# Sparse attention, then Sinkhorn-routed experts on one core: weight loads ordered behind row copies and x, masks and clears moved to GpSimd

## The chip, the cores and the metric

The kernel runs on one core of a Trainium2 chip. The time is device microseconds of one execution, lower is better. The engines are TensorE (PE in the profile; PEld is its weight load), VectorE (DVE), ScalarE (ACT), GpSimd (POOL) and SyncE (SP). DMAs here are issued from the queues of POOL (loads from memory, which also convert f32 to 16 bits), of SP (copies inside the core's memory, transpositions, stores) and at a few places of ACT.

## The reference

Attention over 4 x 8 heads of 768 rows and 64 columns: each query sees the keys closer than 16 rows and a maximum of each block of 32 keys (with the mean of that block's values, weighted by 32). Its result, 3072 rows of 512, goes through eight experts; the gate's probabilities are balanced by eight rounds of row and column scaling.

```python
k_sum = k.reshape(B, H, nb, block, D).max(axis=3)
v_sum = v.reshape(B, H, nb, block, D).mean(axis=3)
mask_l = np.abs(pos[:, None] - pos[None, :]) < window
scores_s = scale * einsum('bhsd,bhnd->bhsn', q, k_sum) + np.log(block)
a = softmax(concat([where(mask_l, scale * q @ k.T, -1e9), scores_s]))
x = matmul(a, concat([v, v_sum]))          # then rows of 512
P = np.exp(x @ w_gate - max)
for _ in range(8):
    P /= P.sum(1, keepdims=True) + 1e-09
    P /= P.sum(0, keepdims=True) + 1e-09
    P *= N / E
for e in range(E):
    out += P[:, e:e + 1] * (np.maximum(x @ w1[e], 0.0) @ w2[e])
```

## The kernel before

**Stages.** Heads go in 16 pairs. Pairs 0 to 3 (the first batch) are done in halves (`pair_half`), pairs 4 to 15 whole (`pair_whole`). Expert 0 is computed as plain matmuls on 384 rows at a time (`hidden0` L221, `project0` L231) while attention runs. Experts 1 to 7 follow in a loop of 80 equal steps with Strassen-like products (L972, L978) whose sums and differences are made on DVE (L919, L922); the first four groups of expert 1 and the eight rounds of scaling (`bridge`, L1159) share the time with the last rows of expert 0.

**Order.** Attention, expert 0 and the bridge are not issued in program order. `Plan` (L35) takes units with an engine, a cost in microseconds, dependences and a priority, and always emits the unit that can start first. So the costs written into `add(...)` decide the order in which each engine's queue is filled; in the run each engine goes through its queue in that order. A unit may have several engines to choose from. DMAs are units of their own: an issue on POOL, a transfer on one "DMA" resource, a landing some time later (`load`, L670); `last[0]` chains all POOL units in a fixed order. `plan.idle` puts filler matmuls (L592) where the plan sees PE free for more than 0.22 us, until the first eviction of expert 0.

**One whole pair** (`pair_whole`, L756). K and Q are transposed (PE, L349; from pair 12 on by a DMA transposition from SP, L354). `key_max` (L370) makes the maxima of 32 keys in three DVE operations (L375 to L377). `block_sums` (PE, L393) and `block_out` (DVE, L399) make the block means of the values in rows 0 to 63 of a tile `V_e`, group 0; L405 spreads them over the other groups. Rows 64 to 127 of `V_e` hold copies of value rows just outside each group of 128: `near_values` (L409), four small DMAs on SP (L414, L416, 10.2 KB each). Scores (PE, L383), exponential (ACT, L429) and band masks (DVE, L435) follow; `edges` (L439) masks the 16 columns on each side of a group into a tile `E_e`, four DVE operations of 32x80. `values` then multiplies: L458 with the own group's values, L464 with `E_e` and `V_e`. `normalize` (DVE, L546 and L547) gives `xs`; x is transposed into `xT` on PE, or for pairs 10 to 14 by a DMA transposition on SP (`x_dma`, L358). There are two `V_e`, two `E_e` and two `xs` tiles, used in turn.

**Clears and constants.** `pads(n)` (L613) clears the gaps of three mask tiles `E_h`; `gate_constants` (L649) casts the identity and the gate's weights; `late_constants` (L653) clears `E_e`, `V_e` and sets `col_en`. All on DVE.

**The end of attention on POOL.** `hold` (L883) copies one element of each of four `qT` tiles to `held`, which makes POOL wait for the Q of pairs 12 to 15; behind it stand the loads of expert 1: four blocks of w1 (`load_w1`, L197, two DMAs each) and w2 (`load_w2`, L208). The sums of those blocks (`w1_sum`, units `Wt` in `bridge`) are DVE units whose dependences in the plan do not name the loads.

Of the kernel before, what the change touches and what calls it, by code (L numbers as in the profile page):

```python
# [10 lines left out]
BF16 = mybir.dt.bfloat16  # L11
# [125 lines left out]
def kernel(  # L137
# [110 lines left out]
    if True:  # L248

        ident = attn.tile([128, 128], BF16, name="ident")  # L250
        held = attn.tile([1, 1], BF16, name="held")
        band = attn.tile([128, LIVE], BF16, name="band")
# [117 lines left out]
        def key_max(i):  # L370
            r = i % NB
            km = attn.tile([128, 1, 24], BF16, tag="km", name="km", bufs=2)
            half = attn.tile([128, 24, 16], BF16, tag="kh", name="kh", bufs=1)
            rows = kT[r][:].rearrange("p (n w) -> p n w", w=32)
            nc.vector.tensor_tensor(out=half[:], in0=rows[:, :, 0:16], in1=rows[:, :, 16:32], op=ALU.max)  # L375
            nc.vector.tensor_tensor(out=half[:, :, 0:8], in0=half[:, :, 0:8], in1=half[:, :, 8:16], op=ALU.max)
            nc.vector.tensor_reduce(out=km[:, 0, :], in_=half[:, :, 0:8], axis=AX.X, op=ALU.max)  # L377
            nc.vector.tensor_tensor(out=ksT[r][:, 0:64].rearrange("p (j n) -> p j n", j=2)[:, :, 0:24],
                                    in0=km[:].to_broadcast([128, 2, 24]), in1=own[:, :, 0:24], op=ALU.mult)
# [16 lines left out]
        def block_out(i):  # L396
            vs = at.pop(("vs", i))
            dst = V_s[i] if i < PB else V_e[i % NE][:, 0, :]
            nc.vector.tensor_tensor(  # L399
                out=dst[0:64].rearrange("p (j x) -> p j x", j=2)[:, :, 0:D],  # L400
                in0=vs[0:64].rearrange("p (j d) -> p j d", j=2),
                in1=own[0:64, :, 24:25].to_broadcast([64, 2, D]), op=ALU.mult)
            if i >= PB:
                ve = V_e[i % NE]
                nc.vector.tensor_copy(out=ve[0:64, 1:G, :],  # L405
                                      in_=ve[0:64, 0:1, :].to_broadcast([64, G - 1, 2 * VD]))

# [31 lines left out]
        def edges(i):  # L439
            ee, er = E_e[i % NE], at.pop(("er", i))  # L440
            for j in range(2):
                q0 = 64 + 32 * j
                nc.vector.tensor_tensor(out=ee[q0:q0 + 32, 0:G - 1, 128 - W:128],
                                        in0=er[0:32, j, 1:G, 0:W],
                                        in1=band[0:32, None, 0:W].to_broadcast([32, G - 1, W]),
                                        op=ALU.mult)
                nc.vector.tensor_tensor(out=ee[q0:q0 + 32, 1:G, 0:W],
                                        in0=er[96:128, j, 0:G - 1, W + 128:LIVE],
                                        in1=band[96:128, None, W + 128:LIVE].to_broadcast([32, G - 1, W]),
                                        op=ALU.mult)  # L450

# [46 lines left out]
        def live(c):  # L498
            return PAD + c * (LIVE + PAD)
# [102 lines left out]
        def band_constants():  # L602

            nc.gpsimd.affine_select(out=band, in_=band, compare_op=ALU.is_ge, fill=0.0,
                                    base=-1, pattern=[[1, LIVE]], channel_multiplier=-1)
            nc.gpsimd.affine_select(out=band, in_=band, compare_op=ALU.is_ge, fill=0.0,
                                    base=2 * W - 1, pattern=[[-1, LIVE]], channel_multiplier=1)

        def ident_constant():
# [3 lines left out]
        def pads(n):  # L613
            t = E_h[n]
            nc.vector.memset(t[:, :, 0:PAD], 0.0)
            nc.vector.memset(t[:, :, live(0):live(HG)].rearrange("p j (g l) -> p j g l", l=LIVE + PAD)[:, :, :, LIVE:],
                             0.0)
            nc.vector.memset(t[:, :, live(HG) + W:], 0.0)

# [28 lines left out]

        def gate_constants():  # L649
            nc.vector.tensor_copy(out=ident16[:], in_=ident[:])  # L650
            nc.vector.tensor_copy(out=wg_bf[:], in_=wg_f32[:])

        def late_constants():  # L653
            def zero(t):
                nc.vector.memset(t, 0.0)

            def ones(t):
                nc.vector.memset(t[0:24, :, D:VD], 32.0 / XS)
                nc.vector.memset(t[32:56, :, VD + D:2 * VD], 32.0 / XS)

            parts = [(0.4, lambda t=t: zero(t[64:128, :, :])) for t in E_e]
            for t in V_e:
                parts += [(0.4, lambda t=t: zero(t[:])), (0.15, lambda t=t: ones(t))]
            return parts + [(0.15, lambda: nc.vector.memset(col_en, float(E) / float(N)))]

# [22 lines left out]
        def pair_start(i, prio):  # L688
# [17 lines left out]
            if i < PB:  # L706
                query_half(i, 0, prio)
            U["km", i] = add("DVE", 0.85, lambda: key_max(i), [U["kT", i, 0]] + war_q[2:], prio)
            if i == 0:
                U["gc"] = add("DVE", 0.35, gate_constants, [U["km", 0]], 0.5)  # L710
# [3 lines left out]
            U["Vs", i] = add("DVE", 0.24 if i < PB else 0.7, lambda: block_out(i), [U["vs", i]],  # L714
                             prio + 0.01, uses=[buf])
# [10 lines left out]
        def pair_half(i, h, prio):  # L726
            if h:
                query_half(i, 1, prio)
            n = PB * h + i
            hold = U["A", PB - 1, 0] if h else None  # L730
            clear = add("DVE", 0.65, lambda: pads(n), [U["km", n - 1]], prio - 0.2) if 0 < n < NEH else None
            buf = Buffer("s")
# [3 lines left out]
            U["mk", i, h] = add("DVE", 0.78, lambda: masks_h(i, h),  # L736
                                [U["X", i, h], U["band"], hist("A", n - NEH), clear], prio)
            tag = "a" if h else "m"
# [17 lines left out]
        def pair_whole(i, prio):  # L756
            U["near", i] = add("SP", 2.5, lambda: near_values(i), [U["v", i], U.get(("A", i - NE, 1))], prio,
                               lag=4.5)
            for h in range(2):
# [5 lines left out]
                                    [U["X", i, h], U.get(("A", i - 2, 1))], prio)  # L765
            U["ed", i] = add("DVE", 0.78, lambda: edges(i),
                             [U["X", i, 0], U["X", i, 1], U["mk", i, 1], U.get(("A", i - NE, 1))], prio)
# [5 lines left out]
            for h in range(2):  # L773
                buf = Buffer("a")
                U["A", i, h] = add("PE", 0.36, lambda h=h: values(i, h),
                                   [U["mk", i, h], U["ed", i], U["sx", i, h], U["Vs", i], U["near", i]],
                                   prio, opens=[buf])
# [49 lines left out]
        def gate(b, xs, prio):  # L827
            buf = Buffer("a")
            U["lg", b] = add("PE", 0.61, lambda: logits(b), xs, prio, opens=[buf])
            U["lo", b] = add("ACT", 0.25, lambda: logits_out(b), [U["lg", b]], prio, uses=[buf])  # L830
# [13 lines left out]
        load_pair(1, "k0")  # L844
        U["band"] = last[0] = add("POOL", 0.7, band_constants, [last[0]])
        load_pair(1, "v")
        load_pair(2, "k0")
        load_pair(3, "k0")
        load_pair(2, "v")
        load_pair(3, "v")  # L850
        zero_w1(0)
        for i in range(PB):
            load_pair(i, "1")
        zero_w1(1)
        load("w2", lambda: load_w2(0), 0.85, 5.2)
        U["gc"] = None
        for i in range(PB):
            pair_start(i, i)
            pair_half(i, 0, i)
        c1 = U["x", PB - 1, 0]  # L860
        for us, fn in late_constants():
            c1 = add("DVE", us, fn, [c1], 12.5)
        expert0(0, [U["x", i, 0] for i in range(PB)])
# [40 lines left out]
    if True:  # L904
# [254 lines left out]
        def bridge():  # L1159
# [54 lines left out]
            for i in range(4):  # L1214
# [8 lines left out]

                op("p1", "PE", 0.44, [], [a])
                op("seed", "ACT", 0.58, ["p1"], [g], [a])
# [133 lines left out]
```

## Time and profile before

| | us |
|---|---|
| median of three runs | 671.15 |
| the runs | 670.29, 671.15, 671.94 |
| the profiled execution | 674.88 |
| its span (first to last instruction) | 673.2 |
| PE busy | 661.4 |
| DVE busy | 581.9 |
| ACT busy | 399.7 |
| POOL busy | 129.5 |

The page lists groups of instructions by line, engine and tile: `out<-in`, shape, count, then busy time and mean duration. Busy time by stage (the first number is the stretch's length, then each engine's busy time with its instructions, the granted TensorE clock, the DMA engines' share and GB/s):

```profile
0.00:15.00 15.00, 13.03 (x166) 7.07 (x168) 11.95 (x84) 9.15 (x15) 13.95 (x24) 1.00 1.43 155
15.00:50.00 35.00, 34.56 (x468) 23.33 (x463) 29.09 (x89) 25.78 (x45) 27.32 (x34) 1.00 1.97 169
50.00:100.00 50.00, 49.27 (x537) 30.44 (x536) 46.06 (x139) 35.32 (x58) 31.38 (x42) 1.00 1.76 129
100.00:150.00 50.00, 46.86 (x348) 26.36 (x347) 35.93 (x104) 27.79 (x53) 6.57 (x11) 0.97 0.46 51
150.00:190.00 40.00, 40.00 (x247) 23.99 (x247) 30.97 (x71) 26.79 (x52) 6.91 (x10) 1.00 0.25 34
```

Attention ends in the fourth stretch; the fifth goes over into the equal steps of experts 1 to 7. The share in the DMA column adds up packets that overlap and can be above 1.

### The profile page before, as it was taken

To read this page: it belongs to the slowest core of one execution; us is meant where nothing else is said; L and a number is where in the kernel's file an instruction comes from. 1 tells how busy PE (TensorE), PEld (TensorE's weight loads), DVE (VectorE), ACT (ScalarE), POOL (GpSimd) and SP (SyncE) were. 2 spreads that over 40 slices of the span, in tenths; PEclk is the share of its full clock that TensorE was granted. 3 is DMA by queue.
4 is the path that set the end of the run, shared out by engine and by line. 5 is a ranking of instruction groups with operands and counts; after the bars stand their busy time and mean duration, and the time that the engine had idled before them with its cause. 6 is when DMAs were issued, how large, how long until landed. Compare 5 with 4: busy or idle time off the path is not lost.

```text
span 673.2 us, 13510 instructions
## 1 busy us (share of the span) xinstructions
PE 661.4 (98%) x5077; PEld 436.4 (65%) x5077; DVE 581.9 (86%) x1475; ACT 399.7 (59%) x782; POOL 129.5 (19%) x175
## 2 busy tenths in 40 slices
PE   8999998999999999999999999999999999999996
PEld 4766655555666666666666666666666666666665
DVE  8889897677799988998799988998899879998885
ACT  6776674565777765555655565555555565556551
POOL 8699440122101010201010010101020101100001
PEclk9999999999999999999999999999999999999999
DMA  9999989000513050311422051305031132201224
GB/s 159 184 150 147 143 97 142 1 1 1 78 11 39 1 79 1 36 14 20 61 23 25 1 79 12 37 1 79 1 36 14 27 52 23 26 1 56 86 80 157
DMA packets 124033, 36.75 MB, mean 55 GB/s; under 512 B 110144, under 2 KB 121152, under 8 KB 123968
## 3 DMA queue, kind: packets, MB, share of 16 engines
q0 software_dynamic: 104128, 25.93, 41.3%
q1 hardware_dynamic: 18880, 9.22, 6.7%
q8 instruction: 40, 0.66, 0.4%
q10 hardware_dynamic: 960, 0.74, 0.3%
q14 instruction: 25, 0.20, 0.1%
HBM read 52.45 MB, written 6.29 MB: 87 GB/s over the span
## 4 chain that ended last, share of the span: by engine, by line
PE 88%; DVE 6%; DMA 5%; issue 0%; ACT 0%; DVEq 0%; ACTq 0%
PE xy L978 37%; PE pg L972 16%; PE pa L972 11%; PE pb L972 11%; PE yps L231 5%; PE hps L221 4%; DMA Ve<-vx 3%; DMA kT<-kst 1%; DVE xs L547 1%; DMA vx<-in_v_dram 1%; PE sg L383 1%; PE tkq L349 1%; PE tx L554 0%; DVE km L377 0%; PE vs L393 0%
## 5 line engine op out<-in xcount | busy, mean ns | idle before, releaser
L978 PEld LDWEIGHTS <-hf 128*128 128x128 f16 x2352 | 230.1, 98 | 95.8 <-issue 0.8
L978 PE MATMUL xy<-w,hf 128*128 128x256 f16 x1312 | 183.4, 273 | 0.0
L978 PE MATMUL xy<-ws,hf 128*128 128x256 f16 x984 | 147.6, 273 | 0.1
L212 ACT ACTIVATE hf<-pg 128x512 f16<-128x512 f32 x84 | 50.1, 597 | 151.3 <-PE pg L972 151.2
L1114 DVE SCALAR_TENSOR_TENSOR out_acc<-xy,P_sb,out_acc 128x512 f32<-128x512 f32 x164 | 115.0, 742 | 2.1 <-PE xy L978 2.1
L919 DVE TENSOR_TENSOR hf<-hf 128x512 f16<-128x512 f16 x252 | 100.2, 425 | 8.9 <-DVE hf L922 0.5
L972 PE MATMUL pa<-xT,w 128*128 128x512 f16 x336 | 99.9, 379 | 0.0
L972 PEld LDWEIGHTS <-w 128*128 128x128 f16 x672 | 65.8, 98 | 43.5
L922 DVE TENSOR_TENSOR hf<-pb,c 128x512 f16<-128x512 f32 x84 | 58.1, 691 | 36.8 <-PE pb L972 34.5
L197 POOL DMA_DIRECT2D w<-in_moe_w_dram x56 | 41.7, 756 | 220.1 <-PE pg L972 191.7
L972 PEld LDWEIGHTS <-ws 128*128 128x128 f16 x504 | 49.3, 98 | 25.1
L1006 ACT COPY c<-pg 128x512 f32<-128x512 f32 x84 | 49.2, 586 | 22.4 <-PE pg L972 22.4
L922 DVE TENSOR_TENSOR hf<-pg,c 128x512 f16<-128x512 f32 x84 | 57.1, 679 | 0.7 <-PE pg L972 0.7
L212 ACT ACTIVATE hf<-pa 128x512 f16<-128x512 f32 x84 | 50.6, 603 | 0.9 <-PE pa L972 0.9
L991 ACT COPY pg<-pa 128x512 f32<-128x512 f32 x84 | 47.9, 570 | 4.9
L972 PE MATMUL pg<-xT,w 128*128 128x512 f16 x168 | 50.0, 379 | 0.0
L972 PE MATMUL pb<-xTs,ws 128*128 128x512 f16 x168 | 50.0, 379 | 0.0
L972 PE MATMUL pg<-xTs,ws 128*128 128x512 f16 x168 | 50.0, 379 | 0.0
L972 PE MATMUL pb<-xT,ws 128*128 128x512 f16 x168 | 50.0, 379 | 0.0
L972 PE MATMUL pg<-xTs,w 128*128 128x512 f16 x168 | 50.0, 379 | 0.0
L999 ACT COPY c<-pb 128x512 f32<-128x512 f32 x84 | 49.8, 593 | 0.0
L221 PE MATMUL hps<-xT,w 128*128 128x384 f16 x256 | 48.9, 326 | 0.0
(150 smaller groups left out, 829.9 us busy)
## 6 DMA issues: line engine op xcount, KB each, us to landing
w<-in_moe_w_dram POOLq DMA_DIRECT2D x8, 1024.0 KB, 9.5
w<-in_moe_w_dram POOLq DMA_DIRECT2D x56, 128.0 KB, 3.4
out_dram<-out_acc SPq DMA_DIRECT2D x20, 256.0 KB, 2.0
vx<-in_v_dram POOLq DMA_DIRECT2D x16, 192.0 KB, 5.8
qst<-in_q_dram POOLq DMA_DIRECT2D x31, 96.0 KB, 5.0
kst<-in_k_dram POOLq DMA_DIRECT2D x24, 96.0 KB, 5.4
w<-in_moe_w_dram POOLq DMA_DIRECT2D x2, 512.0 KB, 9.3
Ve<-vx SPq DMA_DIRECT2D x48, 10.2 KB, 4.6
```

The source lines that it names most:

```text
L197: nc.gpsimd.dma_start(out=t[:, :, h, :], in_=moe_w1[e].rearrange("(dk p) f -> p dk f", p=128)[:, :, f:f + 128])
L212: nc.scalar.activation(out=out, in_=in_, func=AF.Relu, bias=0.0, scale=1.0)
L221: nc.tensor.matmul(hp[:, 0:n], lhsT=w1s[e][:, dk, 128 * f:128 * (f + 1)], rhs=xT[:, dk, t0:t0 + n], start=(dk == 0), stop=(dk == KD - 1))
L231: nc.tensor.matmul(yp[:], lhsT=h[:, f, c * 128:(c + 1) * 128], rhs=w2s[e][:, f, :], start=(f == 0), stop=(f == KF - 1))
L919: nc.vector.tensor_tensor(out=out, in0=in0, in1=in1, op=ALU.subtract)
L922: nc.vector.tensor_tensor(out=out, in0=in0, in1=in1, op=ALU.add)
L972: nc.tensor.matmul(bank[:], lhsT=w[:, dk, :], rhs=x[:, dk, :], start=start and dk == 0, stop=dk == KH - 1, skip_group_check=True)
L978: nc.tensor.matmul(bank, lhsT=a(f)[:, 128 * c:128 * (c + 1)], rhs=w[:, f, :], start=start and f == 0, stop=f == FH - 1, skip_group_check=True)
L991: nc.scalar.copy(out=B["g"][:], in_=B["a"][:])
L999: nc.scalar.copy(out=B["c5"][:], in_=B["b"][:])
L1006: nc.scalar.copy(out=B["c2"][:], in_=B["g"][:])
L1114: nc.vector.scalar_tensor_tensor(out=acc, in0=src, scalar=P_sb[:, t, e:e + 1], in1=acc, op0=ALU.mult, op1=ALU.add)
```

## The change

Five things are changed together.

1. `hold` has more to wait for: the row copies of pair 15, the edges of pair 15 and x of pair 12; the load of w2 waits, in addition, for x of pair 14. The units of expert 1's block sums and first products now name the loads in their dependences.
2. `edges` of pairs 10 to 15 goes from DVE to POOL, with a planned cost of 1.4 us instead of 0.78.
3. `pads(1)`, `pads(2)`, the late clears and the two casts go from DVE to POOL, into the chain of DMA issues.
4. Spreading the block sums is a unit of its own (`Vb`) that the plan may put on ACT or DVE, and from pair 10 on also on POOL.
5. `key_max` makes one reduction over 32 keys in place of two maxima and a shorter reduction.

The planned lag of the row copies goes from 4.5 to 5.3 us.

```diff
         def key_max(i):
-            half = attn.tile([128, 24, 16], BF16, tag="kh", name="kh", bufs=1)
-            rows = kT[r][:].rearrange("p (n w) -> p n w", w=32)
-            nc.vector.tensor_tensor(out=half[:], in0=rows[:, :, 0:16], in1=rows[:, :, 16:32], op=ALU.max)
-            nc.vector.tensor_tensor(out=half[:, :, 0:8], in0=half[:, :, 0:8], in1=half[:, :, 8:16], op=ALU.max)
-            nc.vector.tensor_reduce(out=km[:, 0, :], in_=half[:, :, 0:8], axis=AX.X, op=ALU.max)
+            nc.vector.tensor_reduce(out=km[:, 0, :], in_=kT[r][:].rearrange("p (n w) -> p n w", w=32),
+                                    axis=AX.X, op=ALU.max)
...
-            if i >= PB:
-                ve = V_e[i % NE]
-                nc.vector.tensor_copy(out=ve[0:64, 1:G, :],
-                                      in_=ve[0:64, 0:1, :].to_broadcast([64, G - 1, 2 * VD]))
+        def block_spread(eng, i):
+            ve = V_e[i % NE]
+            rows = ve[0:64, 0:1, :].to_broadcast([64, G - 1, 2 * VD])
+            if eng == "POOL":
+                nc.gpsimd.tensor_copy(out=ve[0:64, 1:G, :], in_=rows)
+            else:
+                copy(eng, ve[0:64, 1:G, :], rows)
...
         def edges(i):
-            ee, er = E_e[i % NE], at.pop(("er", i))
+            ee, er, eng = E_e[i % NE], at.pop(("er", i)), nc.gpsimd if i >= 10 else nc.vector
...
+            nc.gpsimd.tensor_copy(out=ident16[:], in_=ident[:])
...
         def pads(n):
-            t = E_h[n]
+            t, eng = E_h[n], nc.gpsimd if n else nc.vector
...
+        def late_constants(n):
+            if n == 0:
+                nc.gpsimd.tensor_copy(out=wg_bf[:], in_=wg_f32[:])
+                nc.gpsimd.memset(col_en, float(E) / float(N))
+            nc.gpsimd.memset(E_e[n][64:128, :, :], 0.0)
+            nc.gpsimd.memset(V_e[n][:], 0.0)
+            nc.gpsimd.memset(V_e[n][0:24, :, D:VD], 32.0 / XS)
+            nc.gpsimd.memset(V_e[n][32:56, :, VD + D:2 * VD], 32.0 / XS)
...
-                               lag=4.5)
+                               lag=5.3)
...
-            U["ed", i] = add("DVE", 0.78, lambda: edges(i),
+            free = i >= 10
+            U["Vb", i] = add({"ACT": 0.68, "DVE": 0.5, **({"POOL": 0.9} if free else {})}, 0,
+                             lambda: block_spread(U["Vb", i].on, i), [U["Vs", i]], prio)
+            U["ed", i] = add("POOL" if free else "DVE", 1.4 if free else 0.78, lambda: edges(i),
...
-        U["band"] = last[0] = add("POOL", 0.7, band_constants, [last[0]])
+        U["band"] = last[0] = add("POOL", 0.9, band_constants, [last[0]])
         load_pair(1, "v")
         load_pair(2, "k0")
         load_pair(3, "k0")
+        U["pads", 1] = last[0] = add("POOL", 0.7, lambda: pads(1), [last[0]])
         load_pair(2, "v")
         load_pair(3, "v")
+        U["pads", 2] = last[0] = add("POOL", 0.7, lambda: pads(2), [last[0]])
         zero_w1(0)
...
         load("w2", lambda: load_w2(0), 0.85, 5.2)
+        for n in range(NE):
+            U["late", n] = last[0] = add("POOL", 1.2, lambda n=n: late_constants(n), [last[0]])
...
         def hold():
             for r in range(12 % NB, NB):
                 nc.gpsimd.tensor_copy(out=held[0:1, 0:1], in_=qT[r][0:1, W:W + 1])
+            for j in range(2):
+                p = 64 + 32 * j
+                nc.gpsimd.tensor_copy(out=held[p:p + 32, 0:1], in_=V_e[(NP - 1) % NE][p:p + 32, 1, VD * j:VD * j + 1])
+            hold_x(12)
+
+        def hold_x(i):
+            nc.gpsimd.tensor_copy(out=held[0:1, 0:1], in_=xT[0:1, i % PB, i // PB * S:i // PB * S + 1])
 
-        last[0] = add("POOL", 0.3, hold, [last[0]] + [U["kT", i, 1] for i in range(12, NP)])
+        last[0] = add("POOL", 0.6, hold, [last[0], U["near", NP - 1], U["x", 12], U["ed", NP - 1]]
+                      + [U["kT", i, 1] for i in range(12, NP)])
         for i in range(4):
             load(("w1n", i), lambda i=i: load_w1(1, i), 0.85, 1.3)
+        last[0] = add("POOL", 0.2, lambda: hold_x(NP - 2), [last[0], U["x", NP - 2]])
         load("w2n", lambda: load_w2(1), 0.85, 5.0)
...
-                    Wt[i, n] = add("DVE", 0.3, lambda i=i, n=n: w1_sum(1, i, n), [Wt.get((i, n - 1))],
+                    Wt[i, n] = add("DVE", 0.3, lambda i=i, n=n: w1_sum(1, i, n), [Wt.get((i, n - 1)), U["w1n", i]],
                                    980.0 + 5 * i + n)
...
-                op("p1", "PE", 0.44, [], [a])
+                op("p1", "PE", 0.44, [U["w1n", i]], [a])
```

More of the change, by code (lines that the diff above doesn't have):

```diff
@@ L250 @@
         ident = attn.tile([128, 128], BF16, name="ident")
-        held = attn.tile([1, 1], BF16, name="held")
+        held = attn.tile([128, 1], BF16, name="held")
         band = attn.tile([128, LIVE], BF16, name="band")
@@ L439, in edges @@
         def edges(i):
-            ee, er = E_e[i % NE], at.pop(("er", i))
+            ee, er, eng = E_e[i % NE], at.pop(("er", i)), nc.gpsimd if i >= 10 else nc.vector
             for j in range(2):
                 q0 = 64 + 32 * j
[L443 to L450, printed above, removed]
+                eng.tensor_tensor(out=ee[q0:q0 + 32, 0:G - 1, 128 - W:128],
+                                  in0=er[0:32, j, 1:G, 0:W],
+                                  in1=band[0:32, None, 0:W].to_broadcast([32, G - 1, W]),
+                                  op=ALU.mult)
+                eng.tensor_tensor(out=ee[q0:q0 + 32, 1:G, 0:W],
+                                  in0=er[96:128, j, 0:G - 1, W + 128:LIVE],
+                                  in1=band[96:128, None, W + 128:LIVE].to_broadcast([32, G - 1, W]),
+                                  op=ALU.mult)
         def values(i, h):
@@ L613, in pads @@
         def pads(n):
-            t = E_h[n]
[L615 to L618, printed above, removed]
+            t, eng = E_h[n], nc.gpsimd if n else nc.vector
+            eng.memset(t[:, :, 0:PAD], 0.0)
+            eng.memset(t[:, :, live(0):live(HG)].rearrange("p j (g l) -> p j g l", l=LIVE + PAD)[:, :, :, LIVE:], 0.0)
+            eng.memset(t[:, :, live(HG) + W:], 0.0)
         def constants():
@@ L647, in constants @@
                 nc.vector.memset(t[32:56, VD + D:2 * VD], 32.0 / XS)
[L649 to L664, printed above, removed]
+        def late_constants(n):
[6 more added lines that the diff above has]
+            nc.gpsimd.memset(V_e[n][32:56, :, VD + D:2 * VD], 32.0 / XS)
         U = {}
@@ L707, in pair_start @@
                 query_half(i, 0, prio)
-            U["km", i] = add("DVE", 0.85, lambda: key_max(i), [U["kT", i, 0]] + war_q[2:], prio)
-            if i == 0:
-                U["gc"] = add("DVE", 0.35, gate_constants, [U["km", 0]], 0.5)
+            U["km", i] = add("DVE", 1.0, lambda: key_max(i), [U["kT", i, 0]] + war_q[2:], prio)
             buf = Buffer("a")
@@ L713, in pair_start @@
                              [U["v", i]] + ([U.get(("A", i - NE, 1))] if i >= PB else []), prio + 0.01, opens=[buf])
-            U["Vs", i] = add("DVE", 0.24 if i < PB else 0.7, lambda: block_out(i), [U["vs", i]],
+            U["Vs", i] = add("DVE", 0.24, lambda: block_out(i), [U["vs", i]],
                              prio + 0.01, uses=[buf])
@@ L730, in pair_half @@
             hold = U["A", PB - 1, 0] if h else None
-            clear = add("DVE", 0.65, lambda: pads(n), [U["km", n - 1]], prio - 0.2) if 0 < n < NEH else None
             buf = Buffer("s")
@@ L736, in pair_half @@
             U["mk", i, h] = add("DVE", 0.78, lambda: masks_h(i, h),
-                                [U["X", i, h], U["band"], hist("A", n - NEH), clear], prio)
+                                [U["X", i, h], U["band"], hist("A", n - NEH), U.get(("pads", n))], prio)
             tag = "a" if h else "m"
@@ L775, in pair_whole @@
                 U["A", i, h] = add("PE", 0.36, lambda h=h: values(i, h),
-                                   [U["mk", i, h], U["ed", i], U["sx", i, h], U["Vs", i], U["near", i]],
+                                   [U["mk", i, h], U["ed", i], U["sx", i, h], U["Vb", i], U["near", i]],
                                    prio, opens=[buf])
@@ L828, in gate @@
             buf = Buffer("a")
-            U["lg", b] = add("PE", 0.61, lambda: logits(b), xs, prio, opens=[buf])
+            U["lg", b] = add("PE", 0.61, lambda: logits(b), xs + [U["late", 0]], prio, opens=[buf])
             U["lo", b] = add("ACT", 0.25, lambda: logits_out(b), [U["lg", b]], prio, uses=[buf])
@@ L855 @@
         load("w2", lambda: load_w2(0), 0.85, 5.2)
-        U["gc"] = None
+        for n in range(NE):
+            U["late", n] = last[0] = add("POOL", 1.2, lambda n=n: late_constants(n), [last[0]])
+        U["gc"] = U["band"]
         for i in range(PB):
@@ L859 @@
             pair_half(i, 0, i)
-        c1 = U["x", PB - 1, 0]
-        for us, fn in late_constants():
-            c1 = add("DVE", us, fn, [c1], 12.5)
         expert0(0, [U["x", i, 0] for i in range(PB)])
```

## The prediction

> **What bounds the kernel now.** I read the page's busy times first, then the chain of waits, then what TensorE (PE) waited for, then busy time in one-microsecond windows, and last how long single transfers took to land.
>
> ```profile
> span 673.2 us, 13510 instructions
> PE 661.4 (98%) x5077; PEld 436.4 (65%) x5077; DVE 581.9 (86%) x1475; ACT 399.7 (59%) x782; POOL 129.5 (19%) x175
> ...
> PE 88%; DVE 6%; DMA 5%; issue 0%; ACT 0%; DVEq 0%; ACTq 0%
> ```
>
> PE is busy for 98% of the span, so the program can only get shorter where PE stands still, runs at a lowered clock or does filler. From 126 us on the chain is PE matmuls alone, apart from the last few microseconds: experts 1 to 7 repeat a group of 6.08 us (start to start in the chain), which the change does not touch. What it touches is the first 125 us. There the chain lists two long stretches of DMA behind each other:
>
> ```profile
> 98.11 6.43 DMA Ve<-vx
> 104.56 11.35 DMA Ve<-vx
> 115.91 0.14 issue
> 116.04 0.40 PE av L464 x3
> ```
>
> These are the row copies of pairs 14 and 15 (L414/L416). In the list of what PE waited for (100 to 125 us) they are the only large wait, and the windows show its price (columns: PE, PEld, DVE, ACT, POOL busy, granted clock, DMA share, GB/s):
>
> ```profile
> PE av L464 <- DMA Ve<-vx: 2.9, 1, 2.9
> ```
>
> ```profile
> 115.00:116.00 1.00, 0.00 (x0) 0.00 (x0) 0.00 (x0) 0.00 (x0) 0.00 (x0) 1.00 0.99 193
> 116.00:117.00 1.00, 0.96 (x14) 0.79 (x15) 0.49 (x2) 0.00 (x0) 0.00 (x0) 1.00 0.04 6
> 117.00:118.00 1.00, 1.00 (x5) 0.38 (x3) 0.96 (x4) 0.00 (x0) 0.00 (x0) 0.54 0.00 0
> 118.00:119.00 1.00, 1.00 (x4) 0.34 (x3) 0.96 (x5) 0.59 (x1) 0.00 (x0) 0.50 0.00 0
> 119.00:120.00 1.00, 1.00 (x6) 0.56 (x5) 0.96 (x5) 0.00 (x0) 0.00 (x0) 0.50 0.00 0
> 120.00:121.00 1.00, 1.00 (x8) 0.58 (x6) 1.00 (x3) 0.52 (x1) 0.00 (x0) 0.75 0.00 0
> ```
>
> PE waits 2.93 us for the copies. A little later its granted clock halves for a while: 0.46 + 0.50 + 0.50 + 0.25 = 1.71 us of work lost. Together 4.64 us.
>
> Why the copies are late: expert 1's weight loads are issued at 94.54 (L197, eight DMAs) and 100.40 (L208). The same four-DMA copy landed in 1.9 us when issued at 85.8, in 6.5 at 98.1 and in 11.8 at 102.4. The transposition of x (L358) took 2.8 us when issued at 88.42, 6.7 at 96.76, 11.7 at 100.76, 10.8 at 105.44, and 2.7 again at 113.87, when the loads had gone through. VectorE (DVE) stands in that too: its normalisation of pair 14 waits 2.34 us, to 112.58, for the x transposition that frees its buffer, and the edge masks of pair 15 come behind it, at 113.86.
>
> **Part 1, the wait of the weight loads.** POOL now does `hold` after the copies of pair 15, x of pair 12 and the edges of pair 15. With nothing beside them the copies (issued 102.44 to 105.1) land near 105.1 + 1.9 = 107.0 and x of pair 12 near 100.76 + 2.8 = 103.6. Pair 14's normalisation need not wait, DVE reaches pair 15's masks at 110.1 as now (L435 ends at 110.14), and its edges follow. At 112.93, where PE now stops, everything is there. I take all of it: -2.93 and -1.71. The half clock was seen once, in the profiled execution; if the timed ones do not have it only 2.93 is to be had, so the bounds are 2.93 and 4.64.
>
> [...]
>
> What is late next is those loads. Pair 15's edges end near 111.5 on POOL, and the copies of `hold` take seven times 0.21 (L885 mean), to 113. Eight issues at 0.756 end at 119, then the copy that waits for x of pair 14 (its normalisation ends near 111.7, +2.7 = 114.4), then the w2 load, issued by 120. The DMAs of L197 land 3.4 us after issue when alone (7.5 at most in this stretch): the first block near 117, the last near 122.5, and w2 at 120 + 9.0 (its landing at 169.0). DVE's sums of those blocks now start at 117.88 and the first product on PE (pa, L972) at 128.10, that is at 123.5 once 4.6 us are gone. So the covers just hold, but where the loads had 16 us to spare they have about one. The order is planned with 0.85 us of POOL time for a block whose two issues take 1.5, so in DVE's queue a sum can stand up to 4 x 0.65 = 2.6 us before its data, with matmul evictions and the Sinkhorn steps behind it; the first product with P on POOL is queued behind the w2 issue too. PE's filler then is expert 0's last rows (16 x 0.65 of hps, 12 x 0.86 of yps). Bounds 0 and +2.6; I take +0.8, nearer to the covered end because of that filler.
>
> **Part 2, the edge masks.** On DVE four operations a pair, 2 x 0.192 + 2 x 0.196 = 0.78 us, six pairs: 4.7 us less there. On POOL nothing like 32x80 is shown. From below: a 1x1 copy, 0.21. From above: tensor_tensor 128x192 f32, 0.52 to 0.86. The two POOL tensor_tensor sizes (0.52 for 192 elements, 0.726 for 256) would give 3.2 ns an element and 0.16 for 80, under the lower bound; the affine_select rows (0.291 for 128 elements, 0.351 for 160) give 0.20. I take 0.30, 1.2 us a pair against 1.4 in the new plan, so that matmuls placed by the plan find the masks done: 0. The masks end only 0.1 to 0.9 us before PE's use today (pair 13: 101.62 and 101.72), so the cover is the new order, which puts other matmuls ahead by the 1.4; an operation over 0.35 is paid in full.
>
> **Part 3, clears and constants.** From DVE go two `pads` of 0.64 us, 0.43 and 0.36 of casts, and 1.94 of late clears. In the first 20 us DVE is the chain (from 8.79 to 19.74 without a break) and PE does filler (24 matmuls of L592, eight of them at the start). Of the moved work only the `pads` at 12.06 to 12.66 lie on that chain: 0 to -0.6, I take -0.4, since PE's next step also waits for ScalarE. On POOL the clears stand between DMA issues. With 1.9 ns an element (affine_select rows) `pads` is 560 x 1.9 = 1.1 us; two of them and the cast delay the first w1 load from 10.65 to about 13.2. It lands 8.5 us after its issue while 3.4 are needed elsewhere, the queue being full (163 GB/s over 10 to 15 us), so the delay is hidden; uncovered it would be 2.5 - (20.79 - 19.15) = 0.9. The late clears, about 3.7 us, come ahead of pair 4's loads, where POOL now waits 4.0 + 1.9 + 1.7 = 7.6 us for DMA: hidden again. Bounds 0 and +0.9, taken 0.
>
> **Part 4, key maxima and spreading.** Three DVE operations (0.351 + 0.258 + 0.353) become one reduction of 768 elements. Bounds: 0.35 (192 elements) and four times that, 1.4; with 1.05 ns an element (0.691 against 0.557 for 512 and 384 from PSUM) it is 0.353 + 576 x 0.00105 = 0.96, the same as now: 0. The spreading copy (0.483 on DVE, 12 times) may go to ScalarE or POOL; it lies microseconds ahead of its use. The DVE time freed in 60 to 105 us is worth little, because PE waits there only 0.26 + 0.29 + 0.20: 0 to -0.75, taken 0.
>
> **Sum.** -2.93 - 1.71 + 0.8 - 0.4 = -4.24 us. The profiled execution, 673.2 us of span in 674.88, becomes 669.0; the runs' median of 671.15, which the profile exceeds by 3.7, becomes **666.9**. With all terms at their good ends it is 671.15 - 4.64 - 0.6 - 0.75 = 665.2; without the clock term 668.6.
>
> **Rivals.** (a) The stop moves to the weight loads: DVE stands before w1 blocks, evictions stand behind it. For it: the late issues computed above, and x of pair 14 travelling beside them (6.7 instead of 2.7 us). Against: over 20 us of expert 0 filler. Price 2.6 instead of 0.8 and half the clock term lost again: 666.9 + 1.8 + 0.8 = 669.5.
>
> (b) Early loads late: if POOL's clears are not hidden, pair 5's q (issued 30.2, landed 35.7, used at 37.77) slips by the 2.5 + 3.7 us, less 2.1 of margin: 666.9 + 4.1 = 671.0. Against it are the 7.6 us of waiting for DMA.
>
> (c) The slower side: POOL's edge masks are held up by DVE. The P product on POOL took 0.52 us with DVE in single-input or PSUM work and 0.76, 0.77 and 0.86 when a two-input DVE operation on SBUF ran beside it (126.12, 157.55, 155.39). If an edge operation costs 0.65 instead of the planned 0.35, PE stands 24 x 0.30 = 7.2 us: 674.1. It decides from 0.35 + 4.2/24 = 0.53 us an operation. Against it: 80 elements are less than half of 192, and the masks of DVE fill a sixth of the time. [...]
>
> **How the numbers follow.** Forecast 0.60 (own range 665.0 to 668.8), (a) 0.17, (b) 0.08, (c) 0.15. Over 0.3% (2.0 us, about what a measurement of this kernel tells from no change) is outside 669.1 and 673.2. Faster: 0.60 and two thirds of (a), 0.72; same: the rest of (a) and most of (b), 0.13; slower: 0.15. The range leaves out (c) and most of (b) at the top: 664.9 to 670.8.
>
> **What would show it.** In the new profile the waits of PE should have no Ve copy of more than 0.5 us, the clock rows 1.00 from 100 to 130 us, the copies of pair 15 land within 3 us, L197 be issued after 110. Wrong it would be if DVE waits for DMA of w before its block sums with PE idle beside it, if L443/L447 take over 0.5 us on POOL with PE waiting for them at L464, or if PE's first hps at L221 comes later than 21.5 us.

## The result and the profile after

The changed kernel takes 670.27 us (median of 20 runs, 668.43 to 671.34) against 671.56 (20 runs, 670.29 to 674.55) of the kernel before, run beside it: a ratio of 0.9975 [0.9966, 0.9983]. It is faster by a quarter of a per cent, 1.3 us, and in a second set of runs by 0.42% or 2.3 us (0.9958 [0.9943, 0.9973]). Both intervals leave out 1, but the first gain lies within the 0.3% that the prediction counted as no change. The forecast was 4.24 us. The direction held; the size was missed by a factor of 3.3, in the second set of 1.8.

The page of the changed kernel, top and chain of waits:

```profile
span 668.3 us, 13503 instructions
PE 658.5 (99%) x5075; PEld 435.4 (65%) x5075; DVE 571.7 (86%) x1392; ACT 403.9 (60%) x790; POOL 148.0 (22%) x222
...
PE 90%; POOL 4%; DMA 3%; DVE 2%; issue 0%; ACT 0%; DVEq 0%; ACTq 0%
```

The span is 4.9 us shorter than that of the profile before, which would be more than the forecast. But the runs around it don't say so; the pair of profiles does not stand for the pair of kernels. VectorE lost 10 us of work, GpSimd gained 18.5, and PE's share of the chain rose.

What PE waited for in the first 130 us (us in total, times, longest):

```profile
PE idle L593 <- DVE vx L601: 1.1, 1, 1.1
PE tx L555 <- DVE xs L548: 1.1, 3, 0.4
PE tkq L349 <- DMA kst<-in_k_dram: 0.6, 1, 0.6
...
PE av L465 <- POOL Ee L444: 0.2, 1, 0.2
...
PE av L465 <- POOL Ee L448: 0.2, 1, 0.2
```

The wait for a Ve copy is gone. New are 0.6 us for K of pair 4 (its load now stands behind GpSimd's clears) and twice 0.2 for masks made on GpSimd. The windows where the stop was (PE, PEld, DVE, ACT, POOL busy, granted clock, DMA share, GB/s):

```profile
110.00:112.00 2.00, 2.00 (x16) 1.23 (x15) 0.00 (x0) 1.47 (x4) 1.70 (x7) 1.00 0.50 98
112.00:114.00 2.00, 2.00 (x26) 1.29 (x25) 1.41 (x4) 0.49 (x1) 2.00 (x4) 1.00 0.77 74
114.00:116.00 2.00, 2.00 (x11) 0.91 (x10) 0.00 (x0) 0.58 (x1) 2.00 (x4) 1.00 1.38 132
116.00:118.00 2.00, 2.00 (x16) 1.08 (x14) 1.35 (x5) 0.58 (x1) 2.00 (x4) 1.00 1.48 139
```

PE is full and the clock whole. DMA picks up from 112 us: those are expert 1's weights, now behind the copies, which land 1.9 to 3.4 us after their issue. From 112 on POOL does nothing but issue them. So the change does what it says, and the signs that the prediction named for part 1 are there, with one exception: the last of the four copies of pair 15 took 3.4 us where 3 was the mark. Yet most of the 4.64 us did not show in the time.

### The profile page after: what moved, and what is told of

Read it like the earlier page. It is cut to its first block, busy times and chain, and to the rows that moved or that the text cites. A ratio compares the mean times of both kernels' runs of the same rounds, so it can differ in the third digit from the quotient of the medians.

```text
span 668.3 us, 13503 instructions
## 1 busy us (share of the span) xinstructions
PE 658.5 (99%) x5075; PEld 435.4 (65%) x5075; DVE 571.7 (86%) x1392; ACT 403.9 (60%) x790; POOL 148.0 (22%) x222
## 3 DMA queue, kind: packets, MB, share of 16 engines
HBM read 52.45 MB, written 6.29 MB: 88 GB/s over the span
## 4 chain that ended last, share of the span: by engine, by line
PE 90%; POOL 4%; DMA 3%; DVE 2%; issue 0%; ACT 0%; DVEq 0%; ACTq 0%
PE xy L981 37%; PE pg L975 16%; PE pa L975 11%; PE pb L975 11%; PE yps L231 5%; PE hps L221 5%; DMA kst<-in_k_dram 1%; DMA kT<-kst 1%; PE sg L380 1%; POOL qst L324 1%; PE tkq L349 1%; POOL vx L318 1%; PE vs L390 1%; PE ss L471 1%; PE av L465 1%; PE av L459 1%
```

## The experiments

Each was run with the kernel before beside it, in three sets; times are compared within a set where one set has both. Three things were open: whether the stop is as long in ordinary runs as in the profiled one; whether late weight loads give something back; and what the three moves of work do.

**The kernel before, once more.** The same code, profiled again.

> The kernel before, unchanged, for the span and the granted clock of every run. Theory V (the stop before the last row copies is of a different length in each run, and the profiled run of before, 674.88 us, was a long one): spans of 668.5 to 673, most near 669.8, a clock of 0.995 only in the long ones and 0.998 or more in the others. Theory L (the stop is always 4.6 us, and the changed kernel loses 3 us elsewhere): clock 0.995 in nearly all runs.

Measured: 671.90 against 672.08 us, 0.9998 [0.9982, 1.0014]. This profile has a span of 670.3 us instead of 673.2. Its timeline (start, us, instructions, and in brackets what was waited for) and windows at the same place:

```profile
112.97 0.35 PE L458 MATMUL av<-vx,em 128*128 128x65 bf16 x6
114.80 0.48 PE L464 MATMUL av<-Ve,Ee 128*128 128x130 bf16 x3 [1.48 <-DMA Ve<-vx]
```

```profile
114.00:115.00 1.00, 0.20 (x2) 0.13 (x2) 0.00 (x0) 0.00 (x0) 0.00 (x0) 1.00 1.40 157
115.00:116.00 1.00, 1.00 (x15) 0.76 (x15) 0.66 (x2) 0.00 (x0) 0.00 (x0) 1.00 0.57 97
116.00:117.00 1.00, 1.00 (x7) 0.41 (x5) 0.95 (x4) 0.47 (x1) 0.00 (x0) 1.00 0.00 0
117.00:118.00 1.00, 1.00 (x11) 0.65 (x10) 0.94 (x5) 0.39 (x2) 0.00 (x0) 1.00 0.00 0
```

The stop is 1.48 us here, not 2.93, and no half clock follows: 1.00 in every window. The copies landed 8.7 to 10.1 us after their issue, where the prediction's profile had 11.3 to 12.1. Same code, same instructions; what differs is how long the transfers took beside the weight loads. (It can go the other way too: at 7.5 us this profile has a wait of 0.8 us for a load of V that the first did not have.)

Of 91 runs of this kernel over three sets, 13 (6 of 64 in two of them, 7 of 27 in the third) have a mean granted clock of 0.997 or less and take 673.55 to 675.88 us (median 674.12); the other 78 take 669.99 to 673.50 (median 671.49). The profile that the prediction was made from, 674.88 us at a clock of 0.995, is one of the kind that comes once in seven. The theory that the stop varies (V) held: a clock of 0.995 in nearly all runs, as its rival L had it, did not come. The lowered clock goes with the stop: in eight of the kernels here, the changed one among them, no profile has a wait for the copies, and of their 112 runs one has a mean clock of 0.997 or less.

This is the main finding: 1.45 us of stop and 1.71 us of clock, 3.16 of the 4.64 us, were in that one execution and, as far as a profile near the median (672.16 us) can tell, not in the median.

**The wait alone.** The kernel before with the new `hold`, the dependences on the loads that go with it, and nothing else of the change.

```
-        last[0] = add("POOL", 0.3, hold, [last[0]] + [U["kT", i, 1] for i in range(12, NP)])
+        last[0] = add("POOL", 0.6, hold, [last[0], U["near", NP - 1], U["x", 12], U["ed", NP - 1]]
+                      + [U["kT", i, 1] for i in range(12, NP)])
...
+        last[0] = add("POOL", 0.2, lambda: hold_x(NP - 2), [last[0], U["x", NP - 2]])
```

> Only the wait of expert 1's loads (hold, hold_x and the named dependences of block sums and first products), on the kernel before. Theory V: 1.3 to 2.0 us less than before (ratio 0.997 to 0.998), no wait for Ve copies, clock 0.998 or more in every run. Theory L: 4.6 us less (0.993).

Measured: 671.24 us, 0.9988 [0.9975, 1.0], span 669.1. The copies land in 1.9 us, the stop is gone and all 12 runs have a clock of 0.998 or more, but only 0.8 us of time goes with it: less than the 1.3 to 2.0 of theory V, though the interval reaches there, and far from the 4.6 of L. One new wait is in the profile, between 120 and 130 us:

```profile
PE sink L1191 <- DVE csum_sb L1186: 0.5, 1, 0.5
```

There DVE is busy for 9.02 of 10 us, against 6.29 in the second profile of the kernel before and 7.59 in the changed kernel, where this wait isn't there: a little of the crowding that part 1 priced at 0.8.

**The wait left out.** The changed kernel with `hold` as before, so that the loads go behind Q alone.

```
-        last[0] = add("POOL", 0.6, hold, [last[0], U["near", NP - 1], U["x", 12], U["ed", NP - 1]]
-                      + [U["kT", i, 1] for i in range(12, NP)])
+        last[0] = add("POOL", 0.3, hold, [last[0]] + [U["kT", i, 1] for i in range(12, NP)])
...
-        last[0] = add("POOL", 0.2, lambda: hold_x(NP - 2), [last[0], U["x", NP - 2]])
```

> The changed kernel with the loads of expert 1 held back as before (by Q of pairs 12 to 15 alone); everything else as changed. Theory V: like before, 0.999 to 1.001, with the stop before the copies back in its profile. Theory L: 1.0045, slower than before.

Measured: 674.99 us, 1.0048 [1.0028, 1.0068], span 673.3: 0.7% slower than the full change. The theory that the stop varies missed; the number is nearer to its rival's, but neither had the mechanism. What PE waited for, the timeline of POOL and the windows (columns as above) tell why:

```profile
PE av L465 <- POOL Ee L444: 3.0, 1, 3.0
```

```profile
97.50 6.00 POOL L197 DMA_DIRECT2D w<-in_moe_w_dram  x8
103.43 0.96 POOL L208 DMA_DIRECT2D w<-in_moe_w_dram  x1
104.46 0.33 POOL L444 TENSOR_TENSOR Ee<-er,band 32x80 bf16<-32x80 bf16 x1
```

```profile
104.00:106.00 2.00, 0.23 (x1) 0.10 (x1) 0.00 (x0) 0.00 (x0) 1.71 (x5) 1.00 1.58 138
106.00:108.00 2.00, 1.94 (x19) 1.28 (x20) 1.41 (x4) 0.34 (x1) 1.33 (x5) 0.54 2.31 155
108.00:110.00 2.00, 2.00 (x10) 0.95 (x7) 0.56 (x1) 1.31 (x3) 0.00 (x0) 0.61 1.49 196
```

Nine weight-load issues occupy POOL for 6.9 us, and the masks, now on POOL, stand behind them. PE waits 3.0 us for a mask (L465 behind L444), and the clock drops to 0.54. So the wait and the move of the masks belong together: with the masks on GpSimd, PE waits 3.0 us for one when the loads go ahead of them, and twice 0.2 when they go behind. The stop for the copies is not back: PE waits for no copy in this profile, though a w2 load is issued in it at 103.43. It is also a second view of the clock: a 3.0 us stop is followed by a lowered clock, 0.54 and 0.61 over 2 us each, as the 2.93 us one was by 0.50 and 0.54, and six of the seven runs have a mean clock of 0.997 and the seventh 0.995. By the rows, 2 x 0.46 + 2 x 0.39 = 1.70 us of work were lost, against 1.71 in the prediction's profile. The 1.48 us stop was followed by none.

In these three stops the loss came whole (1.71 and 1.70 us) or not at all. In the profile of the clears alone, below, stops of 1.44, 1.23 and 1.40 us were followed by none either: the clock is 1.00 from 100 to 130 us there (the five other runs of that kernel have a mean clock of 0.995 to 0.997). What decides it is not shown.

**Only the w2 load waits.** The kernel before, in which the eight w1 loads go as early as before and the one w2 load alone waits for the copies of pair 15 and x of pairs 12 and 14.

```
+        def hold_rows():
+            for j in range(2):
+                p = 64 + 32 * j
+                nc.gpsimd.tensor_copy(out=held[p:p + 32, 0:1], in_=V_e[(NP - 1) % NE][p:p + 32, 1, VD * j:VD * j + 1])
+            for i in (12, NP - 2):
+                nc.gpsimd.tensor_copy(out=held[0:1, 0:1], in_=xT[0:1, i % PB, i // PB * S:i // PB * S + 1])
...
+        last[0] = add("POOL", 0.8, hold_rows, [last[0], U["near", NP - 1], U["x", 12], U["x", NP - 2]])
```

> On the kernel before, only expert 1's w2 waits (for the copies of pair 15, x of pairs 12 and 14); its w1 blocks start as early as before. Theory P (the copies are slowed by w2's 1024-byte packets, the w1 blocks' 256-byte packets cost them little): the stop at L464 is gone, ratio 0.997 to 0.9985, no worse than waiting with all loads. Rival Q (all loads slow them alike): a stop of 0.5 us or more is left and the ratio is 0.999 to 1.000.

Measured: 670.23 us, 0.9978 [0.997, 0.9987], span 668.9. The copies land in 5.3 to 6.5 us, slower than the 1.9 with all loads held, but in time: L464 follows L458 without a gap.

```profile
113.29 0.35 PE L458 MATMUL av<-vx,em 128*128 128x65 bf16 x6
113.48 0.34 PE L464 MATMUL av<-Ve,Ee 128*128 128x130 bf16 x3
```

The forecast of theory P held; its reason, the size of the packets, was not tested (the first profile of the kernel before has w2 alone in 246 packets for 0.25 MB from 169.5 to 173 us, and w1 in 3168 for 0.79 MB from 200 to 240). So in this kernel it is the w2 load, coming right behind the w1 loads and 2 to 4 us ahead of the copies, that made them too late; the w1 loads alone cost nothing that PE sees. Whether an early w2 load always does it is not shown: the run without the wait has one too (103.43), and no stop for a copy. Holding one transfer gives no less than holding nine gave above (0.9988).

**The clears alone.** The kernel before with pads, late clears and casts on GpSimd.

```
-            t = E_h[n]
-            nc.vector.memset(t[:, :, 0:PAD], 0.0)
+            t, eng = E_h[n], nc.gpsimd if n else nc.vector
+            eng.memset(t[:, :, 0:PAD], 0.0)
...
+        for n in range(NE):
+            U["late", n] = last[0] = add("POOL", 1.2, lambda n=n: late_constants(n), [last[0]])
```

> Only the clears and casts moved from VectorE to GpSimd, on the kernel before. Theory V: 0 to 0.8 us more (ratio 1.000 to 1.001), with a wait of PE for pair 4's K of about 0.6 us as in the changed kernel's profile. Theory L: 3 us more (1.0045).

Measured: 679.13 us, 1.0102 [1.0081, 1.0124], span 675.1, far outside what was expected. The order written out for PE changed with the new costs, and PE reaches pairs 13 to 15 with three stops in place of one:

```profile
108.28 0.38 PE L464 MATMUL av<-Ve,Ee 128*128 128x130 bf16 x3 [1.44 <-DMA Ve<-vx]
...
114.25 0.34 PE L458 MATMUL av<-vx,em 128*128 128x65 bf16 x6 [1.23 <-DVE xs L547]
116.00 0.40 PE L464 MATMUL av<-Ve,Ee 128*128 128x130 bf16 x3 [1.40 <-DMA Ve<-vx]
```

Two of them are for the copies. In the chain behind the last one stand an x transposition of 7.77 us and a row copy of 9.69; in the first profile of the kernel before such transfers took 2.8 and 1.9 us ahead of the weight loads (at 88.42 and 85.8). The third is for DVE's normalisation. None is for a clear.

**The wait and the clears together**, on the kernel before (both edits above).

> The kernel before with two parts, the wait of all loads and the clears on GpSimd. Theory C (the 6.9 us of the clears alone come from row copies and x that meet the loads in another order of the work): with the wait no stop for Ve copies is left and the ratio to before is 0.998 to 1.000. Rival D (the clears cost what they cost, through late loads and GpSimd time): 1.006 or more.

Measured: 672.84 us against 671.92, 1.001 [0.9995, 1.0025], span 670.4. The wait takes some 6 us back from the clears: with it, all three stops are gone. The ratio lies near the 0.998 to 1.000 of theory C and far from the 1.006 of its rival. What is left still lies 0.0012 + 0.001 = 0.2% above the wait alone, across two sets. So the clears on GpSimd cost, and the wait hides most of what they do at 100 to 116 us.

**The clears back on VectorE.** The changed kernel with pads, late clears and casts as in the kernel before; run in two sets.

```
-        for n in range(NE):
-            U["late", n] = last[0] = add("POOL", 1.2, lambda n=n: late_constants(n), [last[0]])
...
+        c1 = U["x", PB - 1, 0]
+        for us, fn in late_constants():
+            c1 = add("DVE", us, fn, [c1], 12.5)
```

> The changed kernel with clears and casts back on VectorE. Theory K (the clears ahead of pair 4's loads cost PE the 0.6 us that it waits for K): ratio to before 0.9965 to 0.997, and no wait for K. Rival (VectorE's relief in the first 30 us outweighs it): 0.998 to 1.000.

Measured: 669.40 us, 0.9969 [0.9957, 0.998], span 667.2. The second time:

> The changed kernel with clears and casts on VectorE, again, beside the changed kernel itself. Theory K: 0.4 to 0.8 us less than the changed kernel (ratio to before 0.9965 to 0.997). Rival: no difference that the intervals can tell.

Measured: 668.90 us, 0.9945 [0.9924, 0.9965], span 667.4. The longest wait for a transfer is no longer there:

```profile
PE idle L593 <- DVE vx L601: 1.1, 1, 1.1
PE ss L471 <- DVE ksT L375: 0.4, 1, 0.4
PE tx L555 <- DVE xs L548: 0.4, 1, 0.4
PE ss L471 <- DVE xs L548: 0.3, 1, 0.3
```

Neither K of pair 4 nor a mask is waited for. Its median lies 0.7 us under that of the changed kernel in the same set, and 0.9 under across two sets. The intervals of the ratios to the kernel before overlap, but run against run, in the same set, it is the faster one in 66 of 70 pairs. It is the fastest version found.

**The changed kernel, once more**, in the set of the run above and of the wait and the clears together.

> The changed kernel, unchanged, beside the others of this call: ratio to before 0.997 to 0.998 by every theory, and no wait for Ve copies in this profile either.

Measured: 669.58 us (668.99 to 670.06), 0.9958 [0.9943, 0.9973], span 668.3. Against the wait and the clears in the same set it lies 3.3 us lower, so masks, key maxima and spreading together did help once the clears are on GpSimd. Which of them is not told apart there. This profile has the copies in time again and no wait for K of pair 4; in its place PE, near the start, waits for expert 0's first weights:

```profile
21.31 0.66 PE L221 MATMUL hps<-xT,w 128*128 128x384 f16 x3 [0.99 <-DMA w<-in_moe_w_dram]
```

Their load stands behind GpSimd's `pads` too (first issue at 13.03 us in the first profile of the change, 10.65 before). So of two profiles of the same kernel one waits 0.6 us for one load behind the clears, the other 1.0 us for another.

**The masks back on VectorE.** The changed kernel with all edge masks on DVE.

```
-            ee, er, eng = E_e[i % NE], at.pop(("er", i)), nc.gpsimd if i >= 10 else nc.vector
+            ee, er, eng = E_e[i % NE], at.pop(("er", i)), nc.vector
```

> The changed kernel with the edge masks of pairs 10 to 15 back on VectorE. Theory R (the masks' move is what the changed kernel has over the wait alone): ratio to before 0.9985 to 0.9995. Rival (the move is worth nothing with the wait there): 0.997 to 0.998, as the changed kernel.

Measured: 670.50 us, 0.9983 [0.9973, 0.9994], span 668.0. This falls between what the two theories had (0.9985 to 0.9995 and 0.997 to 0.998), and it cannot be told from the changed kernel (0.9975 [0.9966, 0.9983], in another set): with the clears on GpSimd, moving the masks is worth nothing that shows, in either direction.

**The late clears moved behind K and Q.** The changed kernel, with the clears of buffer n issued behind the K and Q loads of pair 4 + n instead of ahead of them all.

```
-            load_pair(i)
+            load_pair(i, "kq")
+            if i - PB < NE:
+                U["late", i - PB] = last[0] = add("POOL", 1.2, lambda n=i - PB: late_constants(n), [last[0]])
+            load_pair(i, "v")
```

> The changed kernel with the late clears on GpSimd behind the K and Q loads of pairs 4 and 5 instead of ahead of them. Theory K: no wait of PE for pair 4's K, 0.6 us less than the changed kernel, ratio to before 0.996 to 0.997. Rival (another order of PE eats it): 0.9975 or more.

Measured: 670.31 us, 0.9982 [0.9967, 0.9997], span 667.5. The wait for K of pair 4 is gone, and the time did not fall (0.9975 for the changed kernel, in another set). So the place of the late clears alone doesn't account for their price; the `pads`, which stand ahead of the first weight load, were left on GpSimd here, and no kernel moves them alone.

Another wait is left: here, in both profiles of the changed kernel and with the masks back on VectorE, PE waits 0.36 and 0.34 us for `xs` between 15 and 19 us (part of `PE tx L555 <- DVE xs L548: 1.1, 3, 0.4` above; with the clears on VectorE that line reads `0.4, 1, 0.4`). It does not settle the price either. In the first 20 us PE fills free time with matmuls on zeros, 22 of them in the changed kernel and 27 with the clears on VectorE, and PE's idle time up to 130 us and this filler together are 12.5 us in both profiles of the changed kernel, 11.9 here, and 12.6 and 12.8 with the clears on VectorE. By its waits the fastest kernel would not be the fastest: where the clears cost their 0.7 us stays open.

**Without GpSimd.** The kernel before with the w2 load alone held, the key maximum as one reduction and the spreading as a step of its own on ScalarE or VectorE; clears, casts and all masks stay on VectorE.

```
-            half = attn.tile([128, 24, 16], BF16, tag="kh", name="kh", bufs=1)
...
+            nc.vector.tensor_reduce(out=km[:, 0, :], in_=kT[r][:].rearrange("p (n w) -> p n w", w=32),
+                                    axis=AX.X, op=ALU.max)
...
+            U["Vb", i] = add({"ACT": 0.68, "DVE": 0.5, **({})}, 0,
+                             lambda: block_spread(U["Vb", i].on, i), [U["Vs", i]], prio)
```

> Only w2's load waits; key maxima in one reduction and spreading on ScalarE or VectorE as in the changed kernel; clears, casts and all edge masks on VectorE as before. Theory P with K (the w2 wait carries the gain and the GpSimd work adds nothing): ratio to before 0.9965 to 0.9975. Rival (the masks on GpSimd carry a part): 0.998 or more.

Measured: 669.75 us, 0.9962 [0.9946, 0.9978], span 668.2. Beside the 669.58 of the changed kernel in the same set this is the same time, with no clear, cast or mask moved. But the changed kernel with the clears on VectorE, also in this set, is another 0.85 us faster (668.90; in 81 of 84 pairs of runs). It differs from this one in the wait of all nine loads, the masks and a part of the spreading on GpSimd; which of them gives the 0.85 was not run apart, so that GpSimd's work adds nothing is not shown.

## Why the prediction was right and wrong

**Part 1, the stop: right in its mechanism, wrong in its size, and this is the step that failed.** The prediction wrote: "I take all of it: -2.93 and -1.71. The half clock was seen once, in the profiled execution; if the timed ones do not have it only 2.93 is to be had, so the bounds are 2.93 and 4.64." What the runs showed in its place is 1.48 and 0: a stop half as long in the second profile, and in 78 of 91 runs a mean clock of 0.998 or more, where the executions that lost 1.71 and 1.70 us had 0.995 and 0.997. The term should have read about -1.5. Two runs bear this out: taking away the stop and nothing else was worth 0.8 us with all nine loads held and 1.2 with w2 alone. The lower bound was wrong for the same reason as the value: it doubted the clock but took the length of the stop for fixed. There was a hint: the profiled execution was 3.7 us over the median of the runs, and the sum subtracted from that median what only the longer execution had shown. 671.15 less 1.5, not less 4.64, was the sum to make. That 670.27 lies inside the wide range (664.9 to 670.8) is luck: its top was set by rivals (a) and (b), and neither is what made the gain small. (The stop began at 113.11, which is 116.04 less 2.93, and not at 112.93 as written; nothing hangs on it.)

**Part 1, what is late next: right, and a little too dear.** Eight issues from 111.20 to 117.2 and w2 at 117.36 come some 2 us ahead of the prediction's 119 and 120; the first block sum on DVE starts at 117.09, the first product (pa) at 123.29 (predicted 123.5). PE waits for none of it: 0 in place of +0.8. With the wait alone it was 0.5.

**Part 2, the masks: the term of 0 held, within what the runs resolve.** All but a few operations took near 0.33 us (0.30 was taken):

```profile
L444 POOL TENSOR_TENSOR Ee<-er,band x12: 328/330/976, 80.5 to 108.8; 32x80 bf16<-32x80 bf16 x12
L448 POOL TENSOR_TENSOR Ee<-er,band x12: 330/332/402, 80.9 to 109.3; 32x80 bf16<-32x80 bf16 x12
```

The columns are least, median and greatest ns, and the first and last start. Two 0.2 us waits are all that PE saw of them.

**Part 3, the clears: failed in sign.** The early part gave -0.2 in the first pair of profiles (first hps at 20.40 instead of 20.62) where -0.4 was taken, and nothing in the second (21.31 against 21.32). The part called hidden behind 7.6 us of waiting for DMA was not: K of pair 4 is issued from 22.47 on and PE waits for it, as the chain shows (start, us, engine):

```profile
23.29 8.65 DMA kst<-in_k_dram
31.94 0.14 issue
32.07 0.49 PE tkq L349 x6
```

The other load behind the clears, w1 of expert 0, had been given 0.9 us as its uncovered price and 0 as its value; one profile shows 0, the other 0.99. The measured price of the clears in the changed kernel is 0.7 to 0.9 us, against a predicted gain of 0.4. That it is these waits is not shown: without the wait for K (the late clears moved) the time was no shorter.

**Part 4: taken 0, and nearer its good end.** The reduction of 768 elements takes 0.948 us (0.96 predicted). The spreading as a step of its own and the key maximum together lie 0.7 us of span under the run with only w2 held (668.2 against 668.9), inside the bound of 0 to -0.75; these are single profiles of two sets, so it is a hint.

**The sum, made again from the runs:** -1.5 (stop) + 0 (clock) + 0 (late loads) - 0.2 (early chain) + 0.6 (K, by the first profile) = -1.1 us; -1.3 and -2.3 were measured. Only the first two terms are shown; the 0.6 is a wait of one profile whose removal gave nothing, and what masks, key maxima, spreading and clears do in the order of the work was not separated, so the agreement proves little.

**The rivals.** (a), a stop that moves to the weight loads, did not come in the changed kernel; a little of it, 0.5 us, came in the run with the wait alone. (b), early loads late, came in a small form: K of pair 4 by 0.6 us or the first weights by 1.0, in place of q of pair 5 by 4.1. (c), masks held up by DVE, came in single operations (0.69, 0.98 and 0.82 us, each beside a two-input operation of DVE on SBUF, L436, of 0.54 or 0.55 us), in all about 1.7 us over six pairs, of which PE saw 0.4. Three more masks met such operations (L226, four in a row from 103.05) and took only 0.40, while the four took 0.55 us each instead of the 0.41 of the kernel before: there both engines lost a part. The price of (c), 7.2 us, was not paid: 18 of the 24 masks took 0.33 us. A loss for masks on POOL did come, 3.0 us of stop and 1.70 of clock, but by another way, in the kernel without the wait: 6.9 us of issues ahead of them in POOL's own queue.

## What to carry to other kernels

Before a stall is put into a sum, see whether the profiled execution is an ordinary one: where its time lies over the median of the runs, a wait for contended transfers, and a lowered clock behind it, may be what sets it apart (here 1.45 and 1.71 us), and only the ordinary part can be won. Where several loads delay small copies, hold back only the one that does it; here one of nine transfers gave the whole gain (0.9978 with one held, 0.9988 with nine). When compute moves to the engine that also issues DMAs, count the issues that stand ahead of it in that queue (6.9 us for nine of them here), and the loads that then stand behind it (K of pair 4 waited for by 0.6 us in one profile).

## What the runs showed of the hardware that was not expected

The same small copy took 1.9 us with the weight loads held (the wait alone) and 1.9 to 2.1 ahead of them (at 85.8 us in the first profile of the kernel before), 5.3 to 6.5 behind the w1 loads alone, and 8.7 to 12.1 when issued 2 to 4 us behind a w2 load that followed them. In the kernel before these last copies took 11.3 to 12.1 in one execution and 8.7 to 10.1 in the other. A lowered clock (0.50 and 0.54 over 1 us, 0.54 and 0.61 over 2 us) followed stops of 2.93 and 3.0 us, and none followed those of 1.48 us in the kernel before and of 1.23 to 1.44 in the profile of the clears alone. A GpSimd operation of 0.33 us took 0.69 to 0.98 beside L436 of VectorE, which has two inputs, and 0.40 beside L226, which has two as well and itself took 0.55 us instead of 0.41. One weight load took 0.75 us of GpSimd's time to issue (8 in 6.00, without the wait), more than twice a mask of 32x80 (0.33).
